# Earlier weight loads, a third load buffer and a split first load in a fused retention and MoE kernel

## The chip, the cores and the metric

The kernel runs on one core of one Trainium2 chip. The metric is the device time of one execution in microseconds (us); a median of three runs is given. TensorE (PE) multiplies, VectorE (DVE) and ScalarE (ACT) do the elementwise work, GpSimd (POOL) a little of it, and SyncE (SP) issues all loads and stores.

## What is computed

Three layers in a row, in fp32. First retention: for 4 batches, 8 heads, 576 positions and a head dimension of 64, `scores = q k^T / 8`, multiplied by a decay `gamma^(i-j)` for `j <= i` (0 above the diagonal), and then `ret @ v`. Its output, 2304 tokens by 512, goes through two feed-forward layers:

```python
g = x @ w_gate                      # 512 -> 1536
y = (g * (1 / (1 + exp(-g))) * (x @ w_val)) @ w_out
r = maximum(y @ w_in, 0)            # 512 -> 2048
out = (r * r) @ w_out2
```

The weights arrive as 64-bit floats, so the kernel loads the words and makes fp32 of them on the chip.

## The kernel before

**Products in three parts.** An fp32 operand of the feed-forward layers is split into a rounded `hi` (a cast on ACT) and a rest `lo` (a subtraction on DVE); `three` (line 241) multiplies hi by hi, hi by lo and lo by hi into the same PSUM bank. So every 128x128 by 512 block is three matmuls.

**Weight units.** A unit is a 128x512 block of a weight matrix, 512 KB as 64-bit words. `order` (line 117) numbers them: units 0 to 11 are the gate and value blocks of `f` = 0 to 5 of the first layer, units 12 to 17 its output blocks of the same `f`, then gate, value and output block of each further `f`. `prefetch` (line 124) issues the loads on SP: there are two load buffers (`raw`, pool `raw_p`); if a tile lies in the list `spare` it is a further buffer. `conversion` (line 161) is a generator with five steps a unit: (1) two activations on ACT that wait for the load; (2), (3), (4) a clamp, a shift and a merge on DVE; (5) an addition on DVE, after which the load buffer is free. Step 3 also makes `w_hi` and `w_lo` of the unit before. `pump(k)` runs k steps, up to a limit of five times the units allowed; `ensure` runs as many as a matmul needs. So the place of a `pump` call in the program is the place of the step in the instruction streams of ACT and DVE.

**The attention stage** (lines 376 to 545) runs over 16 pairs of heads, with a lag of two pairs (`LAG`). In iteration n, SP issues the K and V load of pair n+1 and the Q and K load of pair n+2; PE makes the scores of pair n (`s`), applies pair n-2 (`o`, `apply(n-2, False)`), makes the scores of the last chunk, the states (`kvs`) and the last chunk of pair n-2 (again into a bank called `s`). DVE multiplies scores by the mask (`p_sb`, and `pl` for the last chunk) and accumulates states (`sb`); ACT copies results into `xy` and scales K (`prep_state`); in iterations 3 to 6 the first tokens are split into `xh` (ACT) and `xl` (DVE). From iteration 3 on, conversion steps are pumped in between (`FROM - 3`), four in iteration 3 and five in each later one, for 15 units (`UNITS_EARLY`); in iterations 6 to 17 `hidden1_early` multiplies the first 512 tokens with one gate or value unit each. Within this stage all instructions of an engine are issued in program order (`Chained`), so a wait holds everything behind it on its engine. `warm` gives PE four matmuls on ones at the start.

**Afterwards** the feed-forward layers run over five chunks of tokens (`CHUNKS`) and over `f`; a scheduler orders the instructions of each engine here, by program order and what it expects to be ready. Parts of `xy` that are free for a time serve as two further load buffers (`spare.extend`, line 571). The first thing on PE is `out1` of chunk 0 with unit 12, into four banks `a`, which take the place of the attention stage's banks.

The pool `wa_p` holds the `hi` and `lo` tiles of the early units and of six early hidden blocks (`WA` = 21 pairs), `wb_p` the others.

Of the kernel before, what the change touches and what calls it, by code (L numbers as in the profile page):

```python
# [9 lines left out]
F32 = mybir.dt.float32  # L10
# [4 lines left out]
ALU = mybir.AluOpType  # L15
# [6 lines left out]
P = 128  # L22
CC = DM // P
F1 = 1536 // P
F2 = 2048 // P
NC = -(-S // P)
# [10 lines left out]
FROM = 6  # L37

LAG = 2

WA = 21

WARM = 4
UNITS_EARLY = WA - HALF

PUMPS = {0: 1, 1: 4, 2: 1}
# [9 lines left out]
def retention_moe_kernel(  # L56
# [13 lines left out]
    def pool(stack, name, bufs, **kw):  # L70
        return stack.enter_context(
            tc.tile_pool(name=name, bufs=bufs, reuse_waits="tile", **kw)
        )
# [6 lines left out]
    t_p = pool(ctx, "t_p", 2)  # L80
    wa_p = pool(ctx, "wa_p", WA)
    part_p = pool(ctx, "part_p", 1, space=bass.MemoryType.DRAM)
# [5 lines left out]
    def f32(ap):  # L88
        return ap.bitcast(F32)
# [23 lines left out]
    pe, dve, act, pool_e, sp = map(Chained, (nc.tensor, nc.vector, nc.scalar, nc.gpsimd, nc.sync))  # L113
# [6 lines left out]
    raw_t, raw_flat, w_t = {}, {}, {}  # L120
    spare = []
    loads = {"next": 0, "pool": 0, "open": False, "cap": 3 * F1 - 1}

    def prefetch(upto):

        while loads["next"] <= min(upto, len(order) - 1):
            i = loads["next"]
            if loads["pool"] < 2:
                loads["pool"] += 1
                raw_flat[i] = raw_p.tile([P, 1024], U32, tag="raw", name="raw")  # L130
                raw, back = raw_flat[i].rearrange("p (a n) -> p a n", a=2), None
            elif spare:
                back = spare.pop(0)
                raw = back.bitcast(U32)
            else:
                return
            loads["next"] += 1
            ph, what, f = order[i]
            src = (w1, w2)[ph - 1][f, :, ("gvo", "io")[ph - 1].index(what), :].bitcast(U32)
            sp.dma_start(out=raw, in_=src.rearrange("p (a n) -> p a n", a=2))  # L140
            raw_t[i] = raw, back
# [6 lines left out]
    def weight_tiles(early=None):  # L148
        wp = wa_p if early or next(homes) else wb_p
        hi = wp.tile([P, 512], F32R, tag="hi", name="w_hi")  # L150
        lo = wp.tile([P, 512], F32R, tag="lo", name="w_lo")
        return hi, lo
# [51 lines left out]
    def pump(k=1):  # L204
        for _ in range(k):
            if pumped["n"] < pumped["limit"]:
                pumped["n"] += 1
                next(convert, None)
# [10 lines left out]
    def bank(tag):  # L219

        turn[tag] += 1
        home = ps_g2 if late and turn[tag] % 2 else ps_g
        return home.tile([P, 512], F32, tag=tag, name=tag)
# [3 lines left out]
    def split_x(ph, n, cc):  # L227
        t0, m = CHUNKS[ph][n]
        src = xy[:, cc, t0:t0 + m]
        if ph == 2 and n == 0:  # L230
            xs_w.append(weight_tiles())
        if ph == 2 and n % 2 == 0:
            hi, lo = cut(xs_w[cc], 0, m)
        else:
            hi = xs_p.tile([P, N], F32R, tag="xh", name="xh")[:, :m]
            lo = xs_p.tile([P, N], F32R, tag="xl", name="xl")[:, :m]
        act.copy(hi, src)
        dve.tensor_tensor(out=lo, in0=src, in1=f32(hi), op=ALU.subtract)
        xs[ph, n, cc] = (hi, lo)
# [7 lines left out]
    def cut(pair, a, n):  # L247
        return tuple(x[:, a:a + n] for x in pair)
# [127 lines left out]
    with ExitStack() as st:  # L376
        const = pool(st, "const", 1)
# [8 lines left out]
        qk_t, kv_t, q_t, p_t, sb_t, s_t = {}, {}, {}, {}, {}, {}  # L386
        rs = [slice(h * D, (h + 1) * D) for h in range(2)]
        pairs = [(b, hp) for b in range(B) for hp in range(NP)]

        def warm():  # L390

            one = const.tile([P, 256], F32, tag="one", name="one")
            dve.memset(one, 1.0)
            ps = bank("g")
            for _ in range(WARM):
                pe.matmul(ps[:, :256], one[:, :P], one, start=True, stop=True)

        def load_qk(n):
            b, hp = pairs[n]
            qk_t[n] = qk_p.tile([P, 2, S], F32, tag="qk", name="qk_sb")  # L400
            for at in (slice(0, CUT), slice(CUT, S)) if n == 0 else (slice(0, S),):
                sp.dma_start(out=qk_t[n][:, :, at], in_=qk[b, hp][:, :, at])
                if n == 0 and at.start == 0:
                    sp.dma_start(out=ks_sb, in_=kscale)

        def load_kv(n):
            b, hp = pairs[n]
            kv_t[n] = kv_p.tile([P, 2 * NC - 1, P], F32, tag="kv", name="kv_sb")
            sp.dma_start(out=kv_t[n], in_=kv[b, hp])
            if n < NP:  # L410
                sp.dma_start(out=mask_sb[:, n], in_=mask[:, n])
                sp.dma_start(out=qs_sb[:, n], in_=qscale[:, n, P:P + qs_sb.shape[-1]])

        def prep_state(n):
            hp = pairs[n][1]
            for h, r in enumerate(rs):
                kn = kv_t[n][:, NC:, r]
                act.mul(kn, kn, ks_sb[:, hp, 1, h])
            qs = q_p.tile([P, S - P], F32, tag="qs", name="qs")
            for c, m in ((0, 3 * P), (3 * P, D)):  # L420
                w = min(m, P)
                pool_e.tensor_tensor(
                    out=qs[:, c:c + m].rearrange("p (c q) -> p c q", q=w),
                    in0=qk_t[n][:, 0, P + c:P + c + m].rearrange("p (c q) -> p c q", q=w),
                    in1=qs_sb[:, hp, None, :w].to_broadcast([P, m // w, w]), op=ALU.mult,
                )
            q_t[n] = qs

        def width(c):
            return min(P, S - c * P)  # L430
# [43 lines left out]
        def apply(n, last):  # L474

            b, hp = pairs[n]
            cs = (NC - 1,) if last else range(NC - 1)
            if last:
                bank = s_t[min(n + LAG, len(pairs) - 1)][:, 0, 256:256 + D]
            else:  # L480
                bank = ps_o.tile([P, 512], F32, tag="o", name="o")

            def dst(c):
                return bank if last else bank[:, c * P:(c + 1) * P]

            for c in (cs if last else range(1, NC - 1)):
                at = slice((c - 1) * P, (c - 1) * P + width(c))
                for r in rs:
                    pe.matmul(
                        dst(c)[r], sb_t[n][r, c - 1], q_t[n][r, at],  # L490
                        start=(c in (1, NC - 1)), stop=False, skip_group_check=True,
                    )
            for c in cs:
                pt = p_t.pop((n, c))
                for h, r in enumerate(rs):
                    pe.matmul(
                        dst(c)[r], kv_t[n][:, c, r], pt[:, h, :],
                        start=False, stop=True, skip_group_check=True,
                    )
            t0 = b * S + cs[0] * P  # L500
            act.copy(xy[:, hp, t0:t0 + bank.shape[-1]], bank)

        chain["on"] = True
        warm()
        mask_sb = const.tile([P, NP, 2, P], F32, tag="mask", name="mask_sb")
        ks_sb = const.tile([P, NP, NC - 1, 2, 1], F32, tag="ks", name="ks_sb")

# [4 lines left out]
        prep_state(0)  # L512
        last = len(pairs) - 1
        pumped["limit"] = 5 * UNITS_EARLY
        for n in range(last + 1 + LAG):
            new, old, nxt = n <= last, n >= LAG, n + 1 <= last
            fill = PUMPS[0] if n >= FROM - 3 else 0
            if nxt:
                load_kv(n + 1)
            if n + 2 <= last:  # L520
                load_qk(n + 2)
            if n == FROM - 3:
                prefetch(1)
            if new:
                scores(n, range(NC - 1))
            pump(fill if n == FROM - 3 else 2 * fill)
            if old:
                apply(n - LAG, False)
            pump(fill)
            if LAG < n <= LAG + CC:  # L530
                split_x(1, 0, n - LAG - 1)
            if new:
                scores(n, (NC - 1,))
            pump(fill)
            if new:
                states(n)
            pump(fill)
            if FROM <= n < FROM + 2 * HALF:
                hidden1_early(n - FROM)
            if old:  # L540
                apply(n - LAG, True)
            if nxt:
                prep_state(n + 1)
        for cc in range(CC):
            split_x(1, 1, cc)
    chain["on"] = False


    wb_p = pool(ctx, "wb_p", 3 * F1 - WA)
    ps_g2 = pool(ctx, "ps_g2", 1, space=PSUM)  # L550
# [96 lines left out]
```

## Time and profile before

| | us |
|---|---|
| median of 3 runs | 943.98 (943.98 to 945.04) |
| the profiled execution | 942.15 |
| its span in the profile | 940.4 |
| PE busy | 920.8 (98%) |
| weight loads of PE (beside matmuls) | 769.6 (82%) |
| DVE busy | 466.3 (50%) |
| ACT busy | 340.9 (36%) |
| DMA, mean over the span | 67 GB/s |

The profile is one execution. Busy time of PE is modelled at the ends of matmuls. The granted clock of PE is given as a share of 2.4 GHz; its two levels are 1.2 GHz (0.50) and 2.4 GHz (1.00). Nearly all helpers record instructions under line 106 (the chaining wrapper), so groups are told apart by the names of tiles: `out<-in`. In a row of a timeline the bracket at the end gives how long the engine had been idle and what released it.

### The profile page before, as it was taken

The page shows a single profiled execution, that of the slowest core. Times are in us where ns is not written, and L with a number is a line of the kernel's source. Part 1 is how long each engine was busy: PE and PEld are TensorE (multiplying, and loading weights), DVE is VectorE, ACT ScalarE, POOL GpSimd, SP SyncE. Part 2 cuts the span into 40 slices and gives each one's busy share as a digit, 9 for nine tenths or more (in the row PEclk, how much of TensorE's full clock was granted, in tenths as well). Part 3 has the DMA queues.
Part 4 walks back from the last instruction along what each step waited for, and adds up shares of the span by engine and source line. Part 5 has one row for each costly group of instructions (what it writes and reads, how often), then busy time and mean ns, then how long its engine had stood idle before and what let it go on. Part 6 is the DMA issues. An engine that isn't in the chain of part 4 may idle for free.

```text
span 940.4 us, 12525 instructions
## 1 busy us (share of the span) xinstructions
PE 920.8 (98%) x5144; PEld 769.6 (82%) x5144; DVE 466.3 (50%) x845; ACT 340.9 (36%) x629; POOL 21.3 (2%) x39
## 2 busy tenths in 40 slices
PE   8699999999999999999999999999999999999998
PEld 6577778878889998888888888888888888888896
DVE  3688778797424242223899886242224223322332
ACT  2465565554312121112665664232223223222222
POOL 2111100000000000000000000000000000000000
PEclk8799999999999999999999999999999999999999
DMA  8676453542100000001244420000001000100000
GB/s 309 211 249 238 153 157 113 153 137 68 45 1 1 1 2 0 1 1 45 88 136 135 135 90 1 0 34 13 1 1 45 0 1 1 45 1 0 15 31 23
DMA packets 22024, 63.01 MB, mean 67 GB/s; under 512 B 2256, under 2 KB 3792, under 8 KB 21968
## 3 DMA queue, kind: packets, MB, share of 16 engines
q1 hardware_dynamic: 21968, 62.22, 19.6%
q8 instruction: 40, 0.66, 0.3%
q14 instruction: 16, 0.13, 0.0%
HBM read 56.44 MB, written 5.77 MB: 66 GB/s over the span
## 4 chain that ended last, share of the span: by engine, by line
PE 88%; DMA 5%; DVE 4%; ACT 2%; issue 1%; SPq 0%; ACTq 0%
PE a L106 33%; PE g L106 24%; PE v L106 24%; DMA raw<-in_w 3%; PE s L106 3%; PE o L106 3%; DVE w L106 2%; PE kvs L106 1%; DMA xy<-in_w 1%; DVE w_lo L106 1%; DVE t L106 1%; DMA kv_sb<-in_kv 0%; ACT raw L106 0%; DMA part<-part_sb 0%; DVE xl L106 0%
## 5 line engine op out<-in xcount | busy, mean ns | idle before, releaser
L106 ACT ACTIVATE t<-g 128x512 f32<-128x512 f32 (+1 forms) x100 | 55.4, 554 | 211.8 <-PE g L106 211.6
L106 ACT CAST h_hi<-t 128x512 fp32r<-128x512 f32 (+1 forms) x134 | 77.1, 575 | 119.2 <-DVE t L106 113.6
L106 DVE TENSOR_TENSOR h_lo<-t,h_hi 128x512 fp32r<-128x512 f32 (+1 forms) x134 | 85.2, 636 | 67.1 <-ACT h_hi L106 66.7
L106 PE MATMUL v<-xh,w_hi 128*128 128x512 f32 (+1 forms) x304 | 113.8, 374 | 0.0
L106 PE MATMUL g<-xh,w_hi 128*128 128x512 f32 (+1 forms) x304 | 113.8, 374 | 0.0
L106 PE MATMUL g<-xh,w_lo 128*128 128x512 f32 (+1 forms) x304 | 113.3, 373 | 0.0
L106 PE MATMUL v<-xh,w_lo 128*128 128x512 f32 (+1 forms) x304 | 113.2, 373 | 0.0
L106 PE MATMUL g<-xl,w_hi 128*128 128x512 f32 (+1 forms) x304 | 113.2, 372 | 0.0
L106 PE MATMUL v<-xl,w_hi 128*128 128x512 f32 (+1 forms) x304 | 113.2, 372 | 0.0
L106 PE MATMUL a<-w_lo,h_hi 128*128 128x512 f32 x288 | 112.3, 390 | 0.0
L106 PE MATMUL a<-w_hi,h_hi 128*128 128x512 f32 x288 | 112.2, 390 | 0.0
L106 PE MATMUL a<-w_hi,h_lo 128*128 128x512 f32 x288 | 110.1, 389 | 0.0
L106 DVE TENSOR_TENSOR t<-g,t 128x512 f32<-128x512 f32 (+1 forms) x60 | 38.2, 636 | 89.7 <-ACT t L106 89.6
L106 PE MATMUL a<-h_lo,w_hi 128*128 128x512 f32 (+1 forms) x216 | 79.0, 366 | 0.5 <-DVE h_lo L106 0.5
L106 PE MATMUL a<-h_hi,w_lo 128*128 128x512 f32 (+1 forms) x216 | 78.9, 366 | 0.0
L106 DVE SCALAR_TENSOR_TENSOR t<-g,t 128x512 f32<-128x512 f32 (+1 forms) x40 | 25.5, 639 | 105.6 <-ACT t L106 105.4
L106 PE MATMUL a<-h_hi,w_hi 128*128 128x512 f32 (+1 forms) x216 | 76.8, 367 | 0.1
L106 DVE SCALAR_TENSOR_TENSOR t<-v,t 128x512 f32<-128x512 f32 (+1 forms) x40 | 25.6, 639 | 91.7 <-ACT t L106 91.4
L106 DVE TENSOR_SCALAR w<-w 128x512 f32<-128x512 f32 (+1 forms) x136 | 57.4, 423 | 25.9 <-ACT w L106 24.4
L106 PEld LDWEIGHTS g<-xh,w_hi 128*128 128x128 f32 x304 | 57.3, 188 | 10.4 <-issue 0.2
L106 PEld LDWEIGHTS v<-xh,w_hi 128*128 128x128 f32 x304 | 57.3, 188 | 10.2 <-issue 0.2
L106 PEld LDWEIGHTS v<-xh,w_lo 128*128 128x128 f32 x304 | 57.3, 188 | 10.1
(81 smaller groups left out, 1477.6 us busy)
## 6 DMA issues: line engine op xcount, KB each, us to landing
raw<-in_w SPq DMA_DIRECT2D x51, 512.0 KB, 3.6
kv_sb<-in_kv SPq DMA_DIRECT2D x16, 576.0 KB, 4.0
xy<-in_w SPq DMA_DIRECT2D x17, 512.0 KB, 3.7
qk_sb<-in_qk SPq DMA_DIRECT2D x15, 576.0 KB, 5.1
out<-o_sb SPq DMA_DIRECT2D x18, 256.0 KB, 2.2
part<-part_sb SPq DMA_DIRECT2D x4, 256.0 KB, 2.9
xy<-part SPq DMA_DIRECT2D x1, 1024.0 KB, 5.2
mask_sb<-in_mask SPq DMA_DIRECT2D x4, 128.0 KB, 7.3
```

The source lines that it names most:

```text
L106: i = op(*args, **kw)
```

## The change

- The first K and V load (pair 0) is made in two: the K chunks first, then the V chunks (128x512 and 128x640 elements). K of pair 0 is scaled by DVE for the first head and by ACT for the second.
- `warm` runs three matmuls at the start and two more behind the first scores of pair 0.
- The first two weight loads are issued in iteration 2 (`FROM - 4`) instead of 3, and conversion steps are pumped from iteration 4 on (`FROM - 2`) instead of 3.
- A third load buffer, `raw3`, is in the list `spare` during the attention stage; `cap` keeps loads to the units of the stage, and at its end one more step is pumped, all buffers are empty and the third is given up.
- `WA` falls from 21 to 20, so 14 units instead of 15 are converted in the stage.
- In the last iteration, the last chunk of the last pair is applied before `hidden1_early` instead of after it.

```diff
-WA = 21
+WA = 20
-WARM = 4
+WARM = 3
 UNITS_EARLY = WA - HALF
...
-        def warm():
-
-            one = const.tile([P, 256], F32, tag="one", name="one")
-            dve.memset(one, 1.0)
+        def warm(k):
+
             ps = bank("g")
-            for _ in range(WARM):
+            for _ in range(k):
                 pe.matmul(ps[:, :256], one[:, :P], one, start=True, stop=True)
...
-            sp.dma_start(out=kv_t[n], in_=kv[b, hp])
+            for at in (slice(NC, 2 * NC - 1), slice(0, NC)) if n == 0 else (slice(0, 2 * NC - 1),):
+                sp.dma_start(out=kv_t[n][:, at], in_=kv[b, hp][:, at])
...
-                act.mul(kn, kn, ks_sb[:, hp, 1, h])
+                if n or h:
+                    act.mul(kn, kn, ks_sb[:, hp, 1, h])
+                else:
+                    dve.tensor_scalar(out=kn, in0=kn, scalar1=ks_sb[:, hp, 1, h], scalar2=None, op0=ALU.mult)
...
-        warm()
+        one = const.tile([P, 256], F32, tag="one", name="one")
+        dve.memset(one, 1.0)
+        warm(WARM)
...
         pumped["limit"] = 5 * UNITS_EARLY
+        loads["cap"], loads["open"] = UNITS_EARLY - 1, True
+        spare.append(const.tile([P, 2, 512], F32, tag="raw3", name="raw3"))
         for n in range(last + 1 + LAG):
             new, old, nxt = n <= last, n >= LAG, n + 1 <= last
-            fill = PUMPS[0] if n >= FROM - 3 else 0
+            fill = PUMPS[0] if n >= FROM - 2 else 0
...
-            if n == FROM - 3:
+            if n == FROM - 4:
                 prefetch(1)
             if new:
                 scores(n, range(NC - 1))
-            pump(fill if n == FROM - 3 else 2 * fill)
+            if n == 0:
+                warm(2)
+            pump(fill if n == FROM - 2 else 2 * fill)
...
+            if n == last + LAG:
+                apply(n - LAG, True)
             if FROM <= n < FROM + 2 * HALF:
                 hidden1_early(n - FROM)
-            if old:
+            if old and n < last + LAG:
                 apply(n - LAG, True)
...
+        pump(PUMPS[0])
+        assert loads["next"] == UNITS_EARLY and not raw_t
+        loads["cap"], loads["open"] = 3 * F1 - 1, False
+        spare.clear()
```

SP, the loads from the last scales of pair 3 on (`kv_sb`: K and V of a pair, `qk_sb`: Q and K of a pair, `raw` and `raw_138`: weights, the latter in the third buffer), first before, then changed:

```order
L106 DMA qs_sb<-in_qscale 128x161
L106 DMA qk_sb<-in_qk 128x1152
L106 DMA kv_sb<-in_kv 128x1152
L106 DMA qk_sb<-in_qk 128x1152
L106 DMA raw<-in_w 128x1024 x2
```

```order
L106 DMA qs_sb<-in_qscale 128x161
L106 DMA qk_sb<-in_qk 128x1152
L106 DMA raw<-in_w 128x1024 x2
L106 DMA kv_sb<-in_kv 128x1152
L106 DMA qk_sb<-in_qk 128x1152
L106 DMA kv_sb<-in_kv 128x1152
L106 DMA qk_sb<-in_qk 128x1152
L106 DMA raw_138<-in_w 128x1024
```

The first two weight loads move ahead of K and V of pair 4 and of Q and K of pair 5; the third comes behind K and V of pair 5.

DVE, from the mask product of pair 3 (`p_sb`) to the merge of the first unit (`w<-raw,w`), first before, then changed:

```order
L106 TENSOR_TENSOR p_sb<-s,mask_sb 128x1024
L106 TENSOR_SCALAR w<-w 128x512
L106 TENSOR_TENSOR xl<-xy,xh 128x512
L106 TENSOR_TENSOR pl<-s,mask_sb 64x128
L106 TENSOR_SCALAR w<-w 128x512
L106 SCALAR_TENSOR_TENSOR sb<-sb,qs_sb,kvs 128x64 x3
L106 SCALAR_TENSOR_TENSOR w<-raw,w 128x512
```

```order
L106 TENSOR_TENSOR p_sb<-s,mask_sb 128x1024
L106 TENSOR_TENSOR xl<-xy,xh 128x512
L106 TENSOR_TENSOR pl<-s,mask_sb 64x128
L106 SCALAR_TENSOR_TENSOR sb<-sb,qs_sb,kvs 128x64 x3
L106 TENSOR_TENSOR p_sb<-s,mask_sb 128x1024
L106 TENSOR_SCALAR w<-w 128x512
L106 TENSOR_TENSOR xl<-xy,xh 128x512
L106 TENSOR_TENSOR pl<-s,mask_sb 64x128
L106 TENSOR_SCALAR w<-w 128x512
L106 SCALAR_TENSOR_TENSOR sb<-sb,qs_sb,kvs 128x64 x3
L106 SCALAR_TENSOR_TENSOR w<-raw,w 128x512
```

The conversion's rows (`w`) of pair 3 now stand in pair 4; pair 3 has none.

PE, the end of the attention stage (`o` and `s`: the last pair applied, `v`: twelve matmuls of the last `hidden1_early`, `a`: `out1` of unit 12), first before, then changed:

```order
L106 MATMUL v<-xh,w_hi 128x512
L106 MATMUL v<-xl,w_hi 128x512
L106 MATMUL v<-xh,w_lo 128x512
L106 MATMUL s<-qs,sb 64x64 x2
L106 MATMUL s<-pl,kv_sb 64x64 x2
L106 MATMUL a_1596<-w_hi 128x512
```

```order
L106 MATMUL o<-qs,sb 64x128 x6
L106 MATMUL o<-p_sb,kv_sb 64x128 x8
L106 MATMUL s<-qs,sb 64x64 x2
L106 MATMUL s<-pl,kv_sb 64x64 x2
L106 MATMUL v<-xh,w_hi 128x512
L106 MATMUL v<-xl,w_hi 128x512
L106 MATMUL v<-xh,w_lo 128x512
```

The last `s` matmuls now stand ahead of the twelve of `v`, and `a` follows `v` at once. Behind that the compiled order differs too: before, 84 matmuls stand between the first of `a` and the first one with unit 17, in the change 113, because more matmuls of the next chunk stand between the output units.

## Rows read from the trace of the kernel before

**Rows 1.** The page, busy time and granted clock in 40 slices (tenths).

```profile
PE 920.8 (98%) x5144; PEld 769.6 (82%) x5144; DVE 466.3 (50%) x845; ACT 340.9 (36%) x629; POOL 21.3 (2%) x39
...
PEclk8799999999999999999999999999999999999999
```

**Rows 2.** The waits of PE: us in total, times, longest.

```profile
PE s L106 <- DVE pl L106: 9.2, 3, 6.6
PE kvs L106 <- ACT kv_sb L106: 2.4, 1, 2.4
PE a L106 <- ACT xy L106: 1.5, 1, 1.5
```

**Rows 3.** The timeline of pair 3: start, us, engine, out<-in [idle before <-releaser].

```profile
19.41 0.33 SPq L106 DMA_DIRECT2D kv_sb<-in_kv  x1
...
20.05 0.91 ACT L106 ACTIVATE kv_sb<-kv_sb,ks_sb 128x256 f32<-128x256 f32 x2 [0.46 <-DMA kv_sb<-in_kv]
...
22.44 0.69 PE L106 MATMUL kvs<-kv_sb 128*64 128x64 f32 x16
26.51 0.65 ACT L106 ACTIVATE raw<-raw 128x512 uint32<-128x512 uint16 x1 [5.56 <-DMA raw<-in_w]
...
27.62 0.57 ACT L106 COPY xy<-o 128x512 f32<-128x512 f32 x1
...
29.34 0.27 DVE L106 TENSOR_TENSOR pl<-s,mask_sb 64x128 f32<-64x128 f32 x1
...
29.76 0.48 PE L106 MATMUL s<-qs,sb 64*64 64x64 f32 x4 [6.63 <-DVE pl L106]
```

**Rows 4.** Busy time by stretch: us, PE, PEld, DVE, ACT, POOL, clock, DMA.

```profile
9.26:19.26 10.00, 10.00 (x124) 8.58 (x125) 4.77 (x11) 3.39 (x9) 3.04 (x6) 0.67 1.03 397
19.26:30.58 11.32, 4.68 (x77) 3.81 (x73) 4.11 (x11) 3.42 (x8) 1.49 (x3) 0.80 0.57 211
30.58:38.77 8.19, 6.99 (x74) 5.76 (x72) 5.05 (x9) 3.86 (x9) 1.58 (x3) 0.65 0.66 210
38.77:44.50 5.73, 4.39 (x76) 3.62 (x72) 5.35 (x12) 3.90 (x9) 1.30 (x3) 1.00 0.76 251
140.30:160.00 19.70, 19.70 (x89) 16.31 (x88) 16.07 (x30) 10.40 (x19) 0.00 (x0) 1.00 0.36 116
180.00:200.00 20.00, 20.00 (x90) 16.57 (x89) 18.79 (x39) 11.99 (x20) 0.00 (x0) 1.00 0.47 144
220.00:240.00 20.00, 20.00 (x89) 16.55 (x89) 11.18 (x20) 7.87 (x14) 0.00 (x0) 1.00 0.24 79
```

**Rows 5.** The timeline of pair 0.

```profile
1.19 3.78 PE L106 MATMUL g<-one 128*128 128x256 f32 x8 [1.19 <-DVE one L106]
...
7.40 1.28 ACT L106 ACT_TABLE_LOAD   x1 [7.40 <-DMA kv_sb<-in_kv]
...
9.26 1.51 PE L106 MATMUL kvs<-kv_sb 128*64 128x64 f32 x16 [2.38 <-ACT kv_sb L106]
```

**Rows 6.** The timeline around the end of the attention stage, and two conversions.

```profile
127.52 0.67 ACT L106 ACTIVATE raw<-raw 128x512 uint32<-128x512 uint16 x1 [1.98 <-DMA raw<-in_w]
...
129.15 0.22 ACT L106 COPY xy<-s 128x64 f32<-128x64 f32 x1
...
129.43 0.50 PE L106 MATMUL a<-w_hi 128*128 128x512 f32 x1 [1.55 <-ACT xy L106]
...
133.25 0.68 DVE L106 TENSOR_TENSOR w_lo<-w,w_hi 128x512 fp32r<-128x512 f32 x1
...
144.96 0.69 DVE L106 TENSOR_TENSOR w_lo<-w,w_hi 128x512 fp32r<-128x512 f32 x1
```

**Rows 7.** The page, DMA issues: count, KB each, median us to landing.

```profile
raw<-in_w SPq DMA_DIRECT2D x51, 512.0 KB, 3.6
kv_sb<-in_kv SPq DMA_DIRECT2D x16, 576.0 KB, 4.0
...
mask_sb<-in_mask SPq DMA_DIRECT2D x4, 128.0 KB, 7.3
```

## The prediction

> **What bounds the kernel now.** I read the page first: TensorE (PE) is busy 920.8 of 940.4 us and its granted clock is at the upper level (2.4 GHz) from the third of the 40 slices on, so nearly all of the span is matmuls that this change doesn't touch; what can be won is 19.6 us of idle PE and the stretches at the lower level [rows 1]. The list of PE's waits then says whose the idle time is: 9.2 us in three waits of `s` for `pl` on VectorE (DVE), the longest 6.6 us, 2.4 us for the first scaled K, 1.5 us for the last copy into `xy` [rows 2]. All three belong to the attention stage, which ends at 127.88 us.
>
> The timeline of pair 3 shows what is behind the longest. PE's last matmuls before it end at 23.13 us (22.44 + 0.69), and `s` follows at 29.76. It waits for `pl`, which DVE runs at 29.34 in program order, behind `xl`; that needs ScalarE's (ACT's) copy of `o` into `xy` at 27.62, and ACT stood before that for 5.56 us on the first weight load, which landed at 26.51 [rows 3]. So the reader is to see a chain of four in-order queues: DMA, ACT, DVE, PE. The same chain without a weight load to wait for is the other two of the three waits, in pairs 4 and 5: 9.2 - 6.6 = 2.6 us, 1.3 us each [rows 2].
>
> The busy time by stretch, cut at the starts of pairs 1 to 6, shows what the idle time costs afterwards: pair 4 runs 8.19 us at a granted clock of 0.65, pair 5 with the same kind of work 5.73 us at 1.00 [rows 4]. From 9.26 to 19.26 us another thing binds: the DMA share is 1.03 at 397 GB/s, that is, the loads of the first pairs come as fast as they can [rows 4].
>
> **The change, part by part.**
>
> *Weight loads before pair 4's K and V, conversion from pair 4 on.* ACT and DVE no longer meet the first load in pair 3, so `pl` of pair 3 waits only for the rest of the chain. Two bounds for where pair 3 then ends. Late: PE's own position is unchanged (23.13), it waits as in pairs 4 and 5 (1.3), and its last matmuls, 0.82 us at the lower clock (29.76 to 30.58), take about 0.5: 24.9. Early: ACT has scaled pair 3's K by 20.96 (20.05 + 0.91); from the copy of `o` to the end of `pl` it took 1.99 us (27.62 to 29.61), so `pl` is done at 22.95 and pair 3 at 23.5 [rows 3]. I take 24.6, nearer to the row where PE's position is unchanged. Pair 4 then starts at 24.6 instead of 30.58: **-6.0 us** (ends -5.7 and -7.1).
>
> *Pair 4 itself.* With no idle of 6.6 us ahead of it, it should run at the clock that pair 5 has; it now carries the four conversion steps that pair 3 had, no more than pair 5 carries. 8.19 becomes 5.73: **-2.5 us** [rows 4]. The other end is 0, if the clock falls all the same.
>
> *What the moved loads are put in front of.* SP issues in order, and both weight loads now stand ahead of K and V of pair 4 and the Q and K of pair 5. 2 x 512 KB at 397 GB/s are 2.64 us [rows 4]. K and V of pair 4 wait for a buffer that pair 0 frees and were issued at 19.41 [rows 3]; the weights now go ahead of them. 576 KB more at the same rate are 1.49 us, so K and V land at 19.41 + 2.64 + 1.49 = 23.5 at the earliest; since single loads took 4.0 us from issue to landing [rows 7], I take 25. ACT needs 0.91 us for them, and PE uses them some 3.2 us after a pair's start (19.26 to 22.44) [rows 3], that is at 27.8. So I price it at **0**, and the end is +2.64. The third buffer's first load comes behind pair 5's K and V, a pair ahead of its use.
>
> *Pair 0.* The K half comes first and ACT and DVE scale one head each; today ACT starts its table load (1.28 us) when K and V have landed, at 7.40, and PE gets its first `kvs` at 9.26 after 2.38 us idle, followed by ten us at a clock of 0.67 [rows 4, 5]. 320 KB less ahead of K at 397 GB/s are 0.8 us. But five warm matmuls of 0.95 us (3.78 us for four) [rows 5], two of them now behind the first scores, which end at 6.88 (9.26 - 2.38), hold PE until 8.8, and after that pairs 1 to 3 wait for the queue that is full anyway. What they save shows only in pair 3, and is in its early end. **0** for itself.
>
> Here a rule speaks against the split. The loads between 9 and 19 us run at 397 GB/s and a share of 1.03, though half of them are masks of 128 KB and scales that are smaller still [rows 4, 7]. The Trainium skill, DMA: Bandwidth & Descriptors, section Rules for kernel authors, says to coalesce small transfers into large ones, and the table in its section Bandwidth (64 KB in 0.95 us, 1 MB in 6.15 us) would put a fixed part of some 0.6 us on each, an estimate of mine from that page. By it everything behind would come 0.6 us later and the sum would be 9.3 us; by the row it is 9.9. The row decides for me, since the queue shows no such gap between small loads.
>
> *The end of the attention stage.* Now the last pair's `s` matmuls stand behind twelve matmuls of `v`. At 127.88 PE has nothing and waits 1.55 us until ACT's last copy (129.15) frees the PSUM banks of `a`; ACT came to it late because it had stood 1.98 us for a weight load [rows 6]. With `s` ahead of the twelve matmuls (12 x 0.221 = 2.7 us of PE, by 19.70 us for 89 [rows 4]) the copy lies beside them, and ACT reaches the wait for a weight load only behind the copy. I take **-1.4** (ends 0 and -1.55): a small remainder stays for the first output weight, which now has one pair less.
>
> *One unit less, and a restart from empty buffers.* 14 weight units are converted in the stage instead of 15, no load for the 15th is on its way until a buffer and the program allow it, and the third buffer is given back. That moves one unit to a stretch in which PE is full and DVE is at 18.79 of 20 us [rows 4]. Units were 3.9 us apart there (`w_lo` of unit 14 at 133.25, of unit 17 at 144.96) [rows 6]. Before, unit 17's first matmul is the 85th after the first output matmul at 129.43; at 0.221 us each that is 148.0, and `w_lo` is done at 145.65: 2.4 us of slack [rows 4, 6]. A unit later would cost 1.5 us if PE kept its order. It doesn't: the compiled program has 113 matmuls ahead of unit 17 instead of 84, since more matmuls of the next chunk are put between, which gives 29 x 0.221 = 6.4 us more room. So **0**, with +3.9 as the end (one unit's distance, no slack). At the 36th unit DVE has time again (11.18 of 20 us) [rows 4].
>
> **The sum:** -6.0 - 2.5 - 1.4 = -9.9 us. The profiled execution took 942.15 us (span 940.4 and 1.75 around it), so it would take 932.25; the median of the runs shown, 943.98, is 1.83 above it, and I carry that over: **934.1 us**.
>
> **Rivals.**
>
> *The wait moves to K and V of pair 4.* If they land 2.64 us later than I think, PE waits in pair 4 for `kvs`, and then that pair runs at the lower clock as it does today. For it: the queue is full until 19.26 us [rows 4]. Against it: 3 us of distance by the sum above. Price 2.64 + 2.5: the gain shrinks to 4.8, **939.2 us**.
>
> *Slower: the restart from empty buffers starves the output units.* If units 13 to 17 come one load at a time, each is 3.6 us [rows 7] further from the last than the 3.9 us of today, five of them 18 us, with the unit that is missing 21.9; slack and added room are 2.4 + 6.4. PE would stand for 13.1 us, and 2.5 us more go to the lower clock behind it: 15.6 - 9.9 = 5.7 us slower, **949.7 us**. It turns the sign from a distance of 6.4 us a unit on. Against it: two buffers and the parts of `xy` that are freed at once allow loads side by side, and the first of them is issued while the last pair runs.
>
> *It doesn't do what it says.* ACT still meets the weights before they land, only in pair 4 instead of 3, because they share the full queue; then idle time and clock only move by a pair: **943 us**, no difference. Against it: the weights are issued about 5 us earlier and the wait comes a pair later.
>
> **How the numbers follow.** Forecast 0.74, K and V late 0.15, starved units 0.05, nothing gained 0.06. About 0.2% (1.9 us) is what a measurement of this kernel can tell from no change. Faster is the forecast and the K and V case: 0.89; same is the case of nothing gained: 0.06; slower the starved units: 0.05. The range: the favourable ends give 7.1 + 2.5 + 1.55 = 11.2, and if the 1.83 us between profile and median goes too (it may be lower clock in other places), 931; the unfavourable ones without the third rival (5.7 + 2.5 + 0 - 3.9 = 4.3) give 939.7, which takes in the K and V case. I say 930.5 to 940.0.
>
> **What would show it.** Right: no wait of `s` for `pl` above 1.5 us; ACT's wait for the first weights gone; pair 4 starting between 23.5 and 25.0 and pair 6 near 36 instead of 44.50; a granted clock at the upper level from 16 us on; PE going from the last `v` to `a` within 0.3 us; no PE gap above 0.5 us between the end of the stage and 230 us. Wrong: PE waiting for `kvs` in pair 4 or 5, a clock of 0.50 after 20 us, or waits of `a` for `w_hi` or `w_lo` behind the stage.

## The result and the profile after

The changed kernel took **935.05 us** (median of four runs, 934.86 to 936.19) against 943.98 us for the kernel before: a ratio of 0.991 (95% interval 0.9892 to 0.9928). The forecast was 934.1 us. The profiled execution is the slowest of the four, 936.19 us with a span of 934.4 us; the other three have spans of 933.1 to 933.4 us. When the same kernel was run again beside other runs of the kernel before, it took 933.27 us, and the ratio was 0.9905 (0.9889 to 0.992).

The page of the changed kernel, busy time and granted clock in 40 slices, which answers to [rows 1]:

```profile
PE 921.1 (99%) x5146; PEld 768.8 (82%) x5146; DVE 465.9 (50%) x850; ACT 339.5 (36%) x628; POOL 20.6 (2%) x39
...
PEclk9899999999999999999999999999999999999999
```

PE is as busy as before, in a span that is 6.0 us shorter, so its idle time fell from 19.6 to 13.3 us. The list of PE's waits (total, times, longest) says which part went, beside [rows 2]:

```profile
PE s L106 <- DVE pl L106: 4.3, 3, 1.6
...
PE s L106 <- DMA qk_sb<-in_qk: 1.0, 1, 1.0
PE a L106 <- ACT h_hi L106: 0.7, 1, 0.7
...
PE kvs L106 <- ACT kv_sb L106: 0.4, 1, 0.4
```

The wait of 6.6 us is gone and the three that are left are alike (1.34, 1.62 and 1.34 us, in pairs 3 to 5). The wait of 2.4 us for the first K is gone too: the 0.4 us for `kv_sb` stand in pair 1, and 1.0 us for the second part of the first Q and K came in. The wait of `a` for `xy` is not in the list any more. Where the time went after that, the busy time by stretch shows, cut at the starts of pairs 3 to 7 and at the first `a` (columns as in [rows 4]):

```profile
18.59:24.32 5.73, 4.39 (x76) 3.62 (x72) 3.39 (x9) 2.34 (x6) 1.34 (x3) 1.00 1.02 406
24.32:30.34 6.02, 4.40 (x77) 3.62 (x73) 3.33 (x8) 3.34 (x8) 1.28 (x3) 1.00 0.84 285
30.34:37.63 7.29, 5.95 (x75) 4.90 (x72) 5.02 (x10) 3.88 (x9) 1.56 (x3) 0.77 0.79 289
37.63:46.47 8.84, 8.84 (x89) 7.07 (x85) 6.92 (x16) 5.58 (x11) 1.31 (x3) 0.81 0.61 195
46.47:122.41 75.94, 75.94 (x855) 60.15 (x853) 59.50 (x121) 41.05 (x95) 10.90 (x18) 1.00 0.55 187
```

Pair 4 starts at 24.32 us instead of 30.58 and takes 6.02 us instead of 8.19. But pairs 5 and 6, which ran at a granted clock of 1.00 before (5.73 and, from 44.50 to 51.77, 7.27 us), now run at 0.77 and 0.81 and take 7.29 and 8.84 us: 1.56 and 1.57 us are given back. At the first `a`, 122.41 instead of 129.43 us, 7.0 us are won; the rest of the span takes 812.0 us instead of 811.0. (The clock falls once more at 932.3 us, but PE has done its last matmul by 929.8.) So the 6.0 us of the span add up as 6.26 up to the start of pair 4 and 2.17 in it, less 3.13 in pairs 5 and 6, plus 1.7 from there to the first `a`, less 1.0 behind it.

Two engines around pair 4, of the changed kernel's timeline (start, us, engine, operation), answer to [rows 3]:

```profile
25.72 0.91 ACT L106 ACTIVATE kv_sb<-kv_sb,ks_sb 128x256 f32<-128x256 f32 x2 [1.07 <-DMA kv_sb<-in_kv]
...
26.54 0.67 ACT L106 ACTIVATE raw<-raw 128x512 uint32<-128x512 uint16 x1
...
27.50 0.69 PE L106 MATMUL kvs<-kv_sb 128*64 128x64 f32 x16
...
29.81 0.33 PE L106 MATMUL s<-qs,sb 64*64 64x64 f32 x4 [1.62 <-DVE pl L106]
```

ACT takes the first weights (`raw`) without a wait. K and V of pair 4 do come late for ACT, by 1.07 us, but not for PE, whose `kvs` follows at once. Around the end of the stage (answering to [rows 6]; ACT, then PE):

```profile
120.13 0.22 ACT L106 COPY xy<-s 128x64 f32<-128x64 f32 x1
122.25 0.66 ACT L106 ACTIVATE raw<-raw 128x512 uint32<-128x512 uint16 x1 [1.91 <-DMA raw<-in_w]
...
122.19 0.39 PE L106 MATMUL v<-xh,w_lo 128*128 128x512 f32 x1
122.41 0.39 PE L106 MATMUL a<-w_hi 128*128 128x512 f32 x1
```

The last copy into `xy` is done 2 us before `a` needs the banks. ACT still stands 1.91 us for a weight load, now behind the copy.

### The profile page after: what moved, and what is told of

It reads as the page before. It is cut to its first block, busy times and chain, and to the rows that moved or that the text cites. A ratio compares the mean times of both kernels' runs of the same rounds, so it can differ in the third digit from the quotient of the medians.

```text
span 934.4 us, 12527 instructions
## 1 busy us (share of the span) xinstructions
PE 921.1 (99%) x5146; PEld 768.8 (82%) x5146; DVE 465.9 (50%) x850; ACT 339.5 (36%) x628; POOL 20.6 (2%) x39
## 4 chain that ended last, share of the span: by engine, by line
PE 87%; DMA 6%; DVE 4%; ACT 2%; issue 1%; SPq 0%; ACTq 0%
PE a L106 33%; PE g L106 24%; PE v L106 24%; PE o L106 3%; PE s L106 2%; DMA raw<-in_w 2%; DVE w L106 2%; DMA xy<-in_w 2%; DMA kv_sb<-in_kv 1%; PE kvs L106 1%; DVE t L106 1%; DMA part<-part_sb 0%; DVE w_lo L106 0%; SPq L106 0%; ACT w L106 0%
## 5 line engine op out<-in xcount | busy, mean ns | idle before, releaser
L106 PEld LDWEIGHTS g<-xl,w_hi 128*128 128x128 f32 x304 | 57.3, 188 | 10.3 <-DVE xl L106 0.5
```

The costliest lines, as they stand in the source:

```text
L106: i = op(*args, **kw)
```

## The experiments

Two questions were open: which part of the change carries the gain, and why pairs 5 and 6 lost their clock. Each kernel ran in one of three groups, each on one chip with its own runs of the kernel before (medians 943.97, 943.71 and 942.41 us), and the ratios are to these. The changed kernel itself was run again only in the third group; the kernels of the other two have no run of it beside them, so that a small difference of theirs to its 935.05 us proves little.

### The shift alone, and everything but the shift

The first takes the kernel before and shifts load and conversion:

```diff
-            fill = PUMPS[0] if n >= FROM - 3 else 0
+            fill = PUMPS[0] if n >= FROM - 2 else 0
...
-            if n == FROM - 3:
+            if n == FROM - 4:
                 prefetch(1)
...
-            pump(fill if n == FROM - 3 else 2 * fill)
+            pump(fill if n == FROM - 2 else 2 * fill)
```

> The kernel before with one part of the change alone: first weight loads issued two pairs ahead of the first conversion step, conversion one pair later; two load buffers, 15 units, pair 0 and the end of the stage as before. Theory (the shift is the main part): the 6.6 us wait of s for pl in pair 3 shrinks to about 1.3 us, pair 4 starts about 6 us earlier than 30.58, the wait of a for xy at the end of the stage stays at about 1.5 us; 5 to 8 us less than the kernel before (936 to 939 us). Rival (the shift needs the third buffer or the earlier K of pair 0): pair 3 or 4 still waits for the first weights or for K and V, less than 2 us gained (942 us or more).

Measured: 937.32 us (ratio 0.9925, 0.9913 to 0.9937), 6.65 us less than before. Pair 3 takes 5.73 us, pair 4 starts at 24.80, and the wait at the end of the stage is there (windows and PE's waits of this kernel):

```profile
19.07:24.80 5.73, 4.39 (x77) 3.62 (x73) 3.39 (x9) 2.23 (x6) 1.34 (x3) 1.00 1.02 409
```

```profile
PE a L106 <- ACT xy L106: 1.7, 1, 1.7
```

The second takes the changed kernel and makes the same edit backwards:

```diff
-            fill = PUMPS[0] if n >= FROM - 2 else 0
+            fill = PUMPS[0] if n >= FROM - 3 else 0
...
-            if n == FROM - 4:
+            if n == FROM - 3:
                 prefetch(1)
...
-            pump(fill if n == FROM - 2 else 2 * fill)
+            pump(fill if n == FROM - 3 else 2 * fill)
```

> The changed kernel with the shift alone undone: loads and conversion begin together in pair 3, all else as changed. Theory (the shift is the main part): ACT stands for the first load again, pair 4 starts near 30 us, and only the 1.5 us at the end of the stage are left of the gain: 940 to 942.5 us. Rival (the gain is the warm start with the clock at the upper level from 0 us on): at most 1.5 us slower than the changed kernel, 936.5 us or less.

Measured: 941.92 us (ratio 0.9973, 0.9963 to 0.9984), 2.05 us less than before. ACT stands for the first load again, and pair 3 takes 12 us (timeline of ACT, and the window of pair 3):

```profile
26.52 0.65 ACT L106 ACTIVATE raw<-raw 128x512 uint32<-128x512 uint16 x1 [5.23 <-DMA raw<-in_w]
```

```profile
18.57:30.59 12.02, 4.68 (x76) 3.81 (x72) 4.11 (x11) 3.43 (x8) 1.48 (x3) 0.84 0.73 274
```

The two add up: 6.65 + 2.05 = 8.7 us, where the whole change measured 8.93. The shift is the main part and works without the third buffer and without the new pair 0. Both rivals fall.

### Which half of the shift

The changed kernel with its first loads issued a pair later:

```diff
-            if n == FROM - 4:
+            if n == FROM - 3:
                 prefetch(1)
```

> The changed kernel with the first weight loads issued a pair later (in pair 3, where the kernel before has them), conversion still from pair 4 on. Theory (what counts is that conversion does not begin before the load has landed): K and V of pair 4 come earlier, weights land at about 26.5 us, ACT waits for them 1 us at most, within 1 us of 935.05 us. Rival (the earlier load is what counts): ACT stands for the weights in pair 4, s waits for pl 3 us or more, 938 us or more.

Measured: 934.41 us (ratio 0.9889, 0.9868 to 0.9909), not to be told from the changed kernel. PE's instructions are in the same order throughout. ACT takes the weights without a wait here too (SP's issue of the two loads, then ACT):

```profile
21.43 0.95 SPq L106 DMA_DIRECT2D raw<-in_w  x2
...
26.37 0.91 ACT L106 ACTIVATE kv_sb<-kv_sb,ks_sb 128x256 f32<-128x256 f32 x2
27.24 0.69 ACT L106 ACTIVATE raw<-raw 128x512 uint32<-128x512 uint16 x1
```

So what carries the gain here is that the first conversion step comes a pair later; the earlier load adds nothing that shows. One reserve: there was no time to spare. The first load was issued at 21.43 us and landed 5.8 us later, at 27.2, just as ACT came to it, and in this execution ACT came 0.7 us later than in the changed kernel. So a short wait, of up to 0.7 us, could show in another execution. The early load with conversion still in pair 3 was not tried.

### The end of the stage

The changed kernel with the last pair's `s` matmuls behind `v` again:

```diff
-            if n == last + LAG:
-                apply(n - LAG, True)
             if FROM <= n < FROM + 2 * HALF:
                 hidden1_early(n - FROM)
-            if old and n < last + LAG:
+            if old:
                 apply(n - LAG, True)
```

> The changed kernel with the last pair's s matmuls behind the last twelve matmuls of v again. Theory (their place hides ACT's last copy): a waits about 1.5 us for xy at the end of the stage, 936 to 937 us. Rival (the one unit fewer already took ACT's 1.98 us wait for a weight load away, so the copy is early anyway): the wait stays under 0.5 us and the time within 0.5 us of the changed kernel's 935.05 us.

Measured: 935.96 us (ratio 0.9914, 0.9901 to 0.9927); by ratio that cannot be told from the changed kernel, so the time doesn't show the 1.5 us and the trace has to decide. It shows the wait again, and why (ACT, then PE):

```profile
120.60 0.67 ACT L106 ACTIVATE raw<-raw 128x512 uint32<-128x512 uint16 x1 [1.99 <-DMA raw<-in_w]
...
122.22 0.21 ACT L106 COPY xy<-s 128x64 f32<-128x64 f32 x1
...
122.49 0.50 PE L106 MATMUL a<-w_hi 128*128 128x512 f32 x1 [1.54 <-ACT xy L106]
```

ACT stands 1.99 us for a weight load ahead of the copy, although the stage converts one unit less. It is the place of the matmuls that hides the copy, and the rival falls.

### Pair 0 and the third buffer

One kernel has pair 0 as before:

```diff
-WARM = 3
+WARM = 4
...
-            for at in (slice(NC, 2 * NC - 1), slice(0, NC)) if n == 0 else (slice(0, 2 * NC - 1),):
+            for at in (slice(0, 2 * NC - 1),):
...
-                if n or h:
+                if True:
                     act.mul(kn, kn, ks_sb[:, hp, 1, h])
...
-            if n == 0:
-                warm(2)
```

> The changed kernel with pair 0 as before: K and V in one load, both heads scaled on ACT, four warm matmuls ahead and none behind the first scores. Theory (pairs 1 to 3 wait for the full queue anyway): pair 4 starts within 0.7 us of 24.32 us, time within 1 us of 935.05 us. Rival 1 (the split and the warm matmuls carry part of the gain): the clock is at the lower level from about 9 us on, pair 4 starts at 25.3 us or later, 936.5 us or more. Rival 2 (matmuls kept up from 0 us on are what brings the two low stretches at 31.2 and 38.0 us): pairs 5 and 6 run at the upper level, 932 to 933 us.

Measured: 933.37 us (ratio 0.9885, 0.9872 to 0.9898). Another has no third buffer:

```diff
-        spare.append(const.tile([P, 2, 512], F32, tag="raw3", name="raw3"))
```

> The changed kernel without the third load buffer. Theory (loads in the stage are far enough ahead with two buffers, as in the kernel before): within 0.7 us of 935.05 us, pairs 4 to 6 unchanged. Rival (the third buffer keeps ACT from standing for weights): ACT's waits for raw in the stage grow, waits of PE appear in pairs 4 to 8, 936.5 us or more.

Measured: 932.7 us (ratio 0.9872, 0.9852 to 0.9892). In the traces the rivals fall: pair 4 starts at 24.66 and 24.83 us, pair 5 takes 7.29 us in both and pair 6 7.27, PE's waits for `pl` are 4.0 us in all, and without the third buffer ACT waits for weights no longer than 0.3 us ahead of the stage's last copy. But both times came out below the changed kernel's 935.05 us by more than the theory allowed, 1.7 and 2.3 us, and no wait in their traces explains it. So the changed kernel was run again beside one that has both parts undone:

> The changed kernel once more, unaltered, beside the next three on one chip. Theory (the low-clock stretches in the first 45 us fall elsewhere from one execution to the next): the profile shows them at other times than 31.2 and 38.0 us, the time is 935 us within 1.5. Rival (they belong to pairs 5 and 6 of this kernel): the profile shows them at 31 and 38 us again and pairs 5 and 6 take 7.3 and 8.8 us.

> The changed kernel with both pair 0 as before (one load, both heads on ACT, four warm matmuls ahead, none behind the scores) and without the third load buffer. Theory (both parts are worth nothing, the lower times of the two single experiments were those of their chips): within 1 us of the changed kernel run beside it. Rival (each costs what the single experiments showed, about 1.7 and 2.3 us): 1.5 to 4 us less than the changed kernel run beside it.

Measured: the changed kernel 933.27 us, the one without both parts 933.51 us (ratios 0.9905 and 0.9911, intervals 0.9889 to 0.992 and 0.9894 to 0.9927). The first is 1.78 us under 935.05, more than the 1.5 that its theory allowed, and its profile shows no low stretch in pairs 5 and 6 at all. Together the two parts are worth nothing that can be measured; single runs of the two lie between 932.31 and 935.16 us, so that 1 us either way would not show. The unaltered kernel comes down to the times of the two single experiments, so these are no evidence for the edits; part of what differs between executions is the next point.

### Why pairs 5 and 6 lost their clock

The first theory was that the waits of 1.3 to 1.6 us ahead of pairs 5 and 6 bring the clock down. One matmul with an unused result was put into each of the three waits:

```diff
+            if 3 <= n < FROM:
+                warm(1)
             if old and n < last + LAG:
                 apply(n - LAG, True)
```

> The changed kernel with one warm matmul (1.0 us, result unused) ahead of the s matmuls that wait for pl, in pairs 3, 4 and 5. Theory (the low stretches at 31.2 and 38.0 us come from the idle 1.62 and 1.34 us before them): the matmul lies inside the wait and costs nothing, the clock stays at the upper level, pair 5 takes 5.7 us instead of 7.29 and pair 6 7.3 instead of 8.84, 931.5 to 932.5 us. Rival (the low stretches come for another reason): pairs 5 and 6 as in the changed kernel, 935 us or more.

Measured: 932.92 us (ratio 0.988, 0.986 to 0.9899), 0.4 us above the theory's range, with the waits down to 2.2 us and both pairs at the upper level:

```profile
30.07:35.80 5.73, 5.02 (x79) 3.92 (x75) 4.95 (x10) 3.90 (x9) 1.57 (x3) 1.00 0.92 332
35.80:43.07 7.27, 7.27 (x88) 5.76 (x84) 6.82 (x16) 5.60 (x11) 1.29 (x3) 1.00 0.79 269
```

That looks like a proof, and is none: the profile of the unaltered changed kernel, run again, has the three waits in full (first fence) and the same two pairs at 1.00 (second fence, pairs 3 to 6 and the stretch to the first `a`):

```profile
PE s L106 <- DVE pl L106: 4.0, 3, 1.3
```

```profile
18.91:24.64 5.73, 4.39 (x77) 3.62 (x73) 3.39 (x9) 2.34 (x6) 1.36 (x3) 1.00 1.02 409
24.64:30.37 5.73, 4.39 (x77) 3.62 (x73) 3.32 (x8) 3.48 (x8) 1.27 (x3) 1.00 0.87 306
30.37:36.10 5.73, 4.39 (x77) 3.62 (x73) 4.95 (x10) 3.89 (x9) 1.57 (x3) 1.00 0.86 312
36.10:43.37 7.27, 7.27 (x89) 5.76 (x85) 6.82 (x16) 5.59 (x11) 1.29 (x3) 1.00 0.74 252
43.37:119.32 75.95, 75.95 (x857) 60.14 (x853) 59.48 (x121) 41.13 (x95) 10.90 (x18) 1.00 0.55 187
```

And the kernel without the two worthless parts, in the same group, shows the two slow pairs that the first profile had:

```profile
30.35:37.65 7.30, 5.96 (x77) 4.92 (x73) 5.04 (x10) 3.87 (x9) 1.57 (x3) 0.77 0.67 235
37.65:46.48 8.83, 8.83 (x89) 7.06 (x85) 6.91 (x16) 5.59 (x11) 1.29 (x3) 0.81 0.55 194
```

Eight profiles of this study have the later conversion and the waits left as they are. In five of them pair 5 takes 7.3 us, in three 5.73; in two of the five pair 6 takes 8.8 us, in the other six 7.3 at most. In two of the three without it, PE ran at the lower clock earlier instead, within 9 to 18 us. So the waits alone do not decide whether the clock falls: the same program shows the low stretches in one execution and not in another. They cost the first profile 1.56 + 1.57 us. What decides when they come stays open.

### A version that beats both

`s` waits for `pl` of the current pair although it doesn't read it: its output lies in the bank that DVE reads `pl` from. In pairs 0 to 3 the bank of `g` is unused at that time:

```diff
-            if last:
+            if last and n + LAG < FROM:
+                bank = ps_g.tile([P, 512], F32, tag="g", name="g")[:, :D]
+            elif last:
                 bank = s_t[min(n + LAG, len(pairs) - 1)][:, 0, 256:256 + D]
```

> The changed kernel with the s matmuls of pairs 0 to 3 (run in iterations 2 to 5) writing into the bank of g, which is unused until pair 6, instead of the bank that pl of the current pair is read from. Theory (s waits for pl only because both share a bank, and the low clock comes from these waits): the three waits of 4.3 us in all are gone and the clock stays up, pair 7 starts 5 to 7 us earlier than 46.47 us, 928 to 931 us. Rival (another queue is late next): PE waits as long for K, for p_sb or for Q and K instead, at most the 3.1 us of the clock are gained, 932 to 935 us.

Measured: 930.64 us (ratio 0.9856, 0.9834 to 0.9878). The waits for `pl` are gone. The windows of pairs 3 to 6 and the two longest of PE's waits for DVE that are left show what comes next:

```profile
21.18:25.50 4.32, 4.32 (x76) 3.59 (x72) 2.05 (x5) 2.23 (x6) 1.29 (x3) 1.00 0.94 324
25.50:29.82 4.32, 4.32 (x76) 3.59 (x72) 2.89 (x7) 2.54 (x6) 1.72 (x3) 1.00 0.84 251
29.82:34.40 4.58, 4.40 (x77) 3.59 (x73) 3.94 (x10) 3.96 (x10) 1.89 (x3) 1.00 0.93 330
34.40:43.02 8.62, 7.50 (x84) 5.71 (x84) 8.55 (x18) 6.01 (x13) 1.31 (x3) 1.00 0.86 300
```

```profile
PE s L106 <- DVE sb L106: 2.6, 1, 2.6
...
PE kvs L106 <- DVE sb L106: 1.1, 1, 1.1
```

From the start of pair 3 to that of pair 7 it takes 21.84 us, where the changed kernel at the upper clock took 24.46 (18.91 to 43.37). Pairs 3 to 5 win 1.41, 1.41 and 1.15 us, and pair 6 gives 1.35 back, of which 1.1 us are the wait of `kvs`. The place was missed: pair 7 starts 3.45 us before 46.47, not 5 to 7, since pair 3 itself began at 21.18 in this execution. The wait of 2.6 us is in pair 1: DVE stood for the first mask until 10.01 us, and `s` for DVE until 11.94. In the two kernels below, which have the same edit, there is no such wait in pair 1, and pair 3 begins at 18.43 and 19.05. The Trainium skill, PSUM — Partial Sum Buffer, section PSUM bank collisions raise a hardware error, says that an engine that writes a bank and one that reads it must be kept apart on the same partitions even at different columns; the row agrees that the wait went with the bank.

A second bank, that of `v`, was then given to `kvs` of pairs 1, 3 and 5:

```diff
-            ps = ps_o.tile([P, NC - 1, P], F32, tag="kv", name="kvs")[:, :, :D]
+            if n < FROM and n % 2:
+                ps = ps_g.tile([P, 512], F32, tag="v", name="v").rearrange("p (c d) -> p c d", c=NC - 1)[:, :, :D]
+            else:
+                ps = ps_o.tile([P, NC - 1, P], F32, tag="kv", name="kvs")[:, :, :D]
```

> The changed kernel with the s matmuls of pairs 0 to 3 in the bank of g, and kvs of pairs 1, 3 and 5 in the bank of v, both unused then. Theory (with s off the bank, the 1.1 us wait of kvs for sb in pair 6 is again a shared bank): that wait falls under 0.3 us, pair 7 starts about 1 us earlier than the 43.02 us of the kernel with the first bank alone, 929.5 to 930.5 us. Rival (DVE itself is behind, not the bank): another wait of the same length takes its place in pairs 6 to 7, 930.6 us or more.

Measured: 929.54 us (ratio 0.9867, 0.985 to 0.9885). The time lies where the theory had it, but the trace is for the rival (windows of pairs 5 and 6, and two waits of PE):

```profile
27.95:32.90 4.95, 4.39 (x77) 3.59 (x73) 4.88 (x10) 4.14 (x10) 1.93 (x3) 1.00 0.91 352
32.90:41.15 8.25, 7.55 (x84) 5.68 (x85) 8.18 (x18) 5.90 (x13) 0.94 (x3) 1.00 0.68 240
```

```profile
PE g L106 <- DVE xl L106: 0.7, 1, 0.7
PE s L106 <- DVE p_sb L106: 0.6, 1, 0.6
```

The wait of `kvs` for `sb` is gone: `kvs` of pair 6 starts at 36.08 us while DVE still accumulates `sb` of pair 5 (35.74 to 36.64), so this wait too was for a shared bank. But DVE is busy for 8.18 of the 8.25 us of pair 6: it is behind, and gives PE other short waits in place of the one removed. Pairs 3 to 6 take 22.72 us (18.43 to 41.15), no less than the 21.84 with the first bank alone, and the ratios cannot be told apart. Beside it ran the same kernel with pair 0 and the two buffers as before:

> The kernel with both banks and without the two parts that the theory calls worthless: pair 0 as before, no third load buffer. Theory: within 1 us of the kernel with both banks. Rival 1 (the two parts cost): 1.5 to 4 us less, 926 to 928.5 us. Rival 2 (with the waits for banks gone, PE is at the next pair sooner, and an early K of pair 0 or a third buffer is then needed): 1.5 us or more above it, with PE's waits for kv_sb or raw grown.

Measured: 930.03 us (ratio 0.987, 0.9854 to 0.9885), as the theory had it. The two parts are worth nothing here either. The version with two banks is 3.73 us under the changed kernel run beside it (929.54 and 933.27, intervals that don't overlap) and 12.87 us under the kernel before.

## Why the prediction was right, step by step

- **Pair 4 starts earlier, -6.0 us.** Right: -6.26 in the first profile and -5.94 in the second (24.64). ACT no longer meets the load, and the waits that are left have about the length of those in pairs 4 and 5 of before, as the choice "PE's own position is unchanged" had it; PE itself stood 0.67 and 0.35 us earlier than that (22.46 and 22.78 us, against 23.13).
- **Pair 4 at the upper clock, -2.5 us.** Right: -2.17, and -2.46 in the second profile. The 0.3 us between them is the wait of 1.62 us, behind K and V that were 1.07 us late for ACT; it is above the 1.5 us that was said.
- **Pairs 5 and 6.** The step that failed is one that the sum didn't have: it left both at 1.00, as the profile of before showed them. In the first profile they gave 3.13 us back. The reading "With no idle of 6.6 us ahead of it, it should run at the clock that pair 5 has" looked only at pair 4, and took the clock of one execution for the kernel's own. "A granted clock at the upper level from 16 us on" was therefore wrong in one profile and right in the other, up to the last 0.3 us of the span, and pair 6 started at 37.63 in the one and at 36.10 in the other, where "near 36" was said.
- **Loads ahead of K and V of pair 4, 0.** Right: landed about 25.7, forecast 25, used at 27.50. The late load gave the same time. The rival of K and V coming late for PE did not happen.
- **Pair 0, 0.** Right as far as the runs resolve: the kernels with and without it, and the third buffer, are within 0.24 us. In the first profile the first `kvs` came no sooner, at 9.81 us instead of 9.26, behind Q and K that landed later and the two warm matmuls. In the second it came at 8.15, and PE then waited 1.60 us for Q and K of pair 1: the queue took back what K had won, as the prediction had it. The 0.6 us that it drew from the Trainium skill, DMA: Bandwidth & Descriptors, sections Rules for kernel authors and Bandwidth, are an estimate from a table of loads issued by GpSimd, while these are issued by SP, and are below what these runs resolve; no run here decides on that rule.
- **The end of the stage, -1.4 us.** Right, at its early end: the wait of 1.55 us is gone whole, and back with 1.54 us when the matmuls are moved back. A remainder for the first output weight did not appear.
- **One unit fewer, 0.** Right: PE waits for no `w_hi` or `w_lo` behind the stage. From the first `a` to the end of the span it took 811.0 us before, 812.0 and 811.4 us in the two profiles after, 810.0 to 812.6 us in all experiments. The unit was not given back by itself; the kernel with the shift alone has all 15 and takes 812.6. One wait of 0.7 us for `h_hi` in the first profile is above the 0.5 us that was said. The slower rival, starved output units, was far off, and so was that of nothing gained.
- **The sum.** -9.9 us from a profiled 942.15, that is 932.25. The profile with the clock up in pairs 5 and 6 took 932.5 us (span 930.7), the one with it down 936.19 us. The forecast, 934.1, was 0.95 us under the median, and that it came so near is in part luck. The 1.83 us from profile to median were carried over from before, but the two profiles after lie 1.14 us above and 0.77 us below their medians. Without that term the forecast is 2.8 us under 935.05. That lower clock in pairs 5 and 6 of the other executions too makes this up is argued, not shown: they have no profile.

## What to carry to other kernels

When an in-order engine meets a load before it has landed, moving its first use back by one stage can carry the gain by itself, without an earlier load or another buffer; look for whose queue the waiting instruction blocks. A wait for data that the waiting instruction doesn't read can be a shared bank: here another bank took it away, until the next engine was behind. A clock drop in one profile is a sample, so profile the unaltered kernel again before an edit is credited with a clock that stays up.

## What was not expected of the hardware

The granted clock of the same program, with waits in the same places, was 0.77 and 0.81 in pairs 5 and 6 of one execution and 1.00 in both of another. The low level came behind waits of PE of 1.62 and 1.34 us in the one, and did not behind two of 1.34 us in the other. A few microseconds at the lower level cost 1.6 us a pair here, as much as the smaller parts of this change are worth. The Trainium skill, TensorE: Matmul & The Clock Gate, section What's actually happening, says that the same kernel runs a different number of matmuls at the lower clock from run to run, at its start. The two profiles of the changed kernel agree (the two warm matmuls behind the first scores took 2.07 us in the one and 1.13 in the other), and show the same some 25 us later too.
